# Scores of the first batch: float16 halves in place of float32 products in a fused attention and feed-forward kernel

## The chip, the cores and the metric

The kernel runs on one core of one Trainium2 chip. The time is in device microseconds; for each kernel it is the median of several executions. One further execution was recorded by the hardware profiler, and all rows of a profile come from it. The engines are TensorE (PE; its weight loads are listed as PEld), VectorE (DVE), ScalarE (ACT), GpSimd (POOL), and SyncE (SP), whose queue starts all transfers of this kernel. The program gives each engine a fixed list of instructions.

## The reference

```python
# q, k, v: 8 batches x 8 heads x 576 tokens x 64
scores = scale * np.matmul(q, k.transpose(0, 1, 3, 2))       # scale = 1/8
mask = block_i >= block_j                                    # blocks of 64 tokens
...
attn = exp(scores - max) / (sum + 1e-09)
x = (attn @ v), heads side by side                           # 4608 x 512
h = x @ w_in;  g = where(h > 0, h, exp(min(h, 0)) - 1);  x2 = g @ w_out          # 512 -> 2048 -> 512
h = x2 @ w_in2; solu = h * softmax(h); layer norm, * g_ln;  out = ln @ w_out2    # 512 -> 1024 -> 512
```

The weights arrive as float64 and are decoded on the chip from their two 32-bit words.

## The kernel before

**The stages.** Attention and the first feed-forward layer run together: while the feed-forward of batch b runs on TensorE, the attention of batch b + 1 is computed on all engines. The second feed-forward layer follows over 36 tiles of 128 tokens. Two heads make a pair (4 pairs a batch, 32 in all), and a pair has four steps: "01" (query tokens 0 to 255), "2" and "3" (128 each) and "L" (the last 64). Feed-forward works on half a batch at a time, 256 and then 320 tokens: eight products with w_in (24 matmuls each), then eight with w_out.

**Float16 halves.** Most products are computed from a high and a low float16 half of each operand, as three products (high by high, low by high, high by low). For q and k of a pair, `asum_pair` (lines 320 to 324) sums absolute values on ACT, a small matmul with ones adds over partitions (`over_partitions`, L285), `scale_pair` (329) makes the scale on VectorE, `split_hi` (338, ACT) and `split_lo` (344, VectorE) write both halves into the tile N, and `t_pair` (349) transposes N into QKT by five transposing transfers. `Step.mm` (L449, L452, L457) then multiplies.

**The first batch.** Batch 0 doesn't do this: it uses float32. `a_load` (915) brings the first 256 tokens of q and k of all heads, `a_tp` (919) transposes them on TensorE (L925), `a_cp` (928) copies the result to SBUF, and `EarlyStep.mm` (586; L594, L598, mask L600) multiplies in float32. This "pass over the first 256 tokens" gives step 01 of all four pairs at once. The steps 2, 3 and L of a pair follow with `load_early`, `e_tp` (L665) and `e_cp`. After the softmax, batch 0 stays in float32 in any case: `norm` (L610, POOL), transposes of the probabilities on TensorE (L619), and products with v (L637).

**The weights.** w_in is decoded in four groups of two pieces (`wi_*`): load, absolute value on ACT (L773), sign on POOL (L777), clamp and bit operations on VectorE (L780, L784, L785), a sum on TensorE (L844), the scale (L848), then a high half on ACT (L794) and a low half on VectorE or POOL (L798, L800). w_out follows in eight groups (`wo_*`) by the same steps. The raw words of w_out are staged in memory that w_in's decoding uses (the tile XT), so those loads wait until w_in is done. A draining of the feed-forward (`g1_act`, L693) needs the scales of all of w_in.

**The order.** Nothing in the program is dynamic. Each operation is handed to a planner (`Plan`) with an engine, a cost, a due time (`nom`) and what it depends on; the planner simulates the engines, always takes the ready operation with the earliest due time, and the instructions are written in that order. Due times come from the numbers in TUNE: w_in's group g is due at T_WI + g * D_WI, w_out's at T_WO + d * D_WO, step n of attention at `tick(n)`, the feed-forward of batch 0 at T_M0 and T_M1. STAY is how much TensorE prefers to stay with attention or with feed-forward, BACK how long after its scores a product with v is due. Buffers are rings: L and QKT have two, N one, the PSUM tiles m four. All feed-forward products form one chain in fixed order.

Of the kernel before, what the change touches and what calls it, by code (L numbers as in the profile page):

```python
# [29 lines left out]
STAY, SWITCH = 15.6, 0.11  # L30
# [6 lines left out]
SC_IN, SC_OUT, CP, ECP, GMODE, GREST = "PPAPVPVV", "VPVPPPPV", "ACT", "ACT", "PPPPPPPPPPPPPPPP", "D"  # L37
TUNE = (4.41, 8.8, 11.93, 45.41, 10.32, 10.31, 48.22, 7.08, 26.77, 46.96, 6.41, 119.81, 5.28, 10.45, 14.76, 22.34, 7.51, 12.81)
SLACK = {"PE": 0.0, "DVE": 0.0, "ACT": 0.15, "Pool": 0.1, "SP": 0.1}
KINDS = ("01", "2", "3", "L")  # L40
EARLY = 1
# [159 lines left out]
def kernel(  # L201
# [51 lines left out]
    eighth = const.tile([128, 1], F32, name="eighth")  # L253
# [35 lines left out]
    def consts():  # L289
        P.memset(mkA[:, 0:64], 2.0 ** 57)  # L290
        P.memset(mkA[:, 64:128], 0.0)
        P.memset(mkB, -(2.0 ** 57))
        P.memset(ones, 1.0)
        P.memset(ones32, 1.0)
        make_identity(nc, ident)
        P.memset(eighth, 0.125)
# [4 lines left out]
    def l_tails():  # L301
        for i in range(2):
            P.memset(L[i][64:128, :, 4], 0.0)
# [269 lines left out]
    class EarlyStep(Step, Out):  # L573
# [12 lines left out]
        def mm(s):  # L586
            s.e_tile()
            s.S = mtile(s.slot)
            qt = s.qk()
            for a in range(2):  # L590
                r = slice(64 * a, 64 * a + 64)
                if s.kind == "L":
                    for c0, c1, bank in ((0, 512, 0), (512, 576, 1)):
                        E.matmul(out=s.S[r, bank, 0:c1 - c0], lhsT=qt[r, 0, 512:576], rhs=qt[r, 1, c0:c1], start=True, stop=True)  # L594
                else:
                    for i in s.tiles:
                        n = 128 * (i + 1)
                        E.matmul(out=s.S[:, a, s.off[i]:s.off[i] + n], lhsT=qt[r, 0, 128 * i:128 * i + 128], rhs=qt[r, 1, 0:n],  # L598
                                 start=True, stop=False)
                        E.matmul(out=s.S[:, a, s.off[i] + n - 64:s.off[i] + n], lhsT=mkA, rhs=mkB, start=False, stop=True)  # L600

# [40 lines left out]

    def qkt_tile():
        return att.tile([128, 4, 576], F16, name="QKT", tag="QKT", bufs=2).rearrange("p c n -> p (c n)").bitcast(F32)

    tp_t = {}

    def load_early(p):
        h0 = 2 * p
        for w, src in enumerate((q, k)):  # L650
            t = 0 if w else 2
            for h in range(2):
                SP.dma_start(out=L[p % 2][:, w, t:4, h, :],
                             in_=src[0, h0 + h, 128 * t:512, :].rearrange("(t p) d -> p t d", p=128))
            SP.dma_start(out=L[p % 2][0:64, w, 4], in_=src[0, h0:h0 + 2, 512:576, :].rearrange("h p d -> p h d"))

    def e_tp(p, w, slot):
        if p not in qkt_t:
            qkt_t[p] = qkt_tile()[:, 0:1152].rearrange("p (s n) -> p s n", s=2)
            sc_t[p] = (None, eighth)  # L660
        tp_t[p, w] = mtile(slot).rearrange("p a n -> p (a n)")
        lo = 2 if p < 4 and w == 0 else 0
        for t in range(lo, 5):
            r = 128 if t < 4 else 64
            E.transpose(tp_t[p, w][:, 128 * t:128 * t + r], L[p % 2][0:r, w, t].rearrange("p h d -> p (h d)"), ident[0:r, 0:r])  # L665

    def e_cp(p, w):
        c = slice(256 if p < 4 and w == 0 else 0, 576)
        move("ACT" if w == 0 else ECP, qkt_t[p][:, w, c], tp_t[p, w][:, c])
# [242 lines left out]
    LA = [t.rearrange("p s t h d -> p (s t h d)")[:, 0:1024].rearrange("p (t j c) -> p t j c", t=2, j=4) for t in L]  # L912
    qa_t = {}

    def a_load(j, w, t):
        SP.dma_start(out=LA[w][:, t, 2 * j:2 * j + 2].rearrange("p z (h d) -> p (z h) d", h=2),
                     in_=(q, k)[w][0, 4 * j:4 * j + 4, 128 * t:128 * t + 128, :].rearrange("h p d -> p h d"))

    def a_tp(j, slot):
        qa_t[j] = qkt_tile()[:, 0:1024].rearrange("p (z s n) -> p z s n", z=2, s=2)  # L920
        tp_t[j] = mtile(slot, (128, 2, 2, 256))
        for z in range(2):
            for t in range(2):
                for w in range(2):
                    E.transpose(tp_t[j][:, z, w, 128 * t:128 * t + 128], LA[w][:, t, 2 * j + z], ident)  # L925

    def a_cp(j, z):
        move("ACT" if z == 0 else "DVE", qa_t[j][:, z], tp_t[j][:, z])


# [44 lines left out]
    def plan_all(fn, nom, o):  # L975
# [4 lines left out]

    a_ld = [[op("SP", DMA_IN, lambda j=j, w=w, t=t: a_load(j, w, t), -9 + j, dma=dL(131072, 256)) for w in range(2) for t in range(2)]
            for j in range(2)]
# [3 lines left out]


    a_T, a_last = [], []
    for j in range(2):
        d = rM.take()  # L990
        o = op("PE", 8 * cE(256), lambda j=j, d=d: a_tp(j, d), 5 + j, a_ld[j], d, rQKT.take(), o_const)
        a_last.append(o)
        c = op("ACT", cA(512, 0, 0, True), lambda j=j: a_cp(j, 0), 6 + j, o)
        c2 = op("DVE", cV(512), lambda j=j: a_cp(j, 1), 6 + j, o, c)
        rM.use(c, c2)
        a_T.append([c, c2])
    o_tails = op("Pool", 0.3, l_tails, 10, a_last)


# [133 lines left out]
    def plan_early(s, nom, Ts):  # L1133
        if s.kind == "L":
            c, parts = 1.4 * 4 * cE(576) + 0.1, [576]
        else:
            c = 1.4 * sum(2 * 4.05 * cE(128 * (i + 1)) + 2 * cE(64) for i in s.tiles)
            parts = [128 * (i + 1) for i in s.tiles for a in range(2)]
# [128 lines left out]
    for j in range(4):  # L1267
        gen.append((T_A + 3 * j, 0, ("A", j)))
    n = 0
    tq = {}  # L1270
    for p in range(NP):
        for kind in KINDS[1:] if p < 4 else KINDS:
            gen.append((tick(n), 0, ("S", p, kind)))
            tq.setdefault(p, tick(n))
            n += 1
    tm = 0.0
    for b in range(B):
        for i in range(32):
# [28 lines left out]
    def plan_pair_load(p, t):  # L1307
        d = [o_tails] + a_last if p < 2 else o_prep[p - 2]
        o_ld[p] = op("SP", 6 * DMA_IN, lambda: load_early(p), t, d, dma=dL(458752, 256))
        event(t + LEAD - 12, plan_pair_early, p)  # L1310

    def plan_pair_early(p, t):
        cs = []
        for w in range(2):
            nt = 3 if p < 4 and w == 0 else 5
            z = rM.take()
            o = op("PE", nt * cE(256), lambda w=w, z=z: e_tp(p, w, z), t + w, o_ld[p], z, rQKT.take() if w == 0 else o_prep[p][0])
            o_prep.setdefault(p, []).append(o)
            n = 320 if p < 4 and w == 0 else 576
            if w == 0:  # L1320
                c = op("ACT", cA(n, 0, 0, True), lambda w=w: e_cp(p, w), t + w + 0.5, o)
            else:
                c = op(ECP, cA(n, 0, 0, True) if ECP == "ACT" else cV(n), lambda w=w: e_cp(p, w), t + w + 0.5, o, cs[:1])
            z.users.append(c)
            cs.append(c)
        o_T[p] = cs
        q_users[p] = rQKT.users[-1]
# [26 lines left out]
    for t, _, g in gen:  # L1354
        run_backs(t)
        if g[0] == "A":
            j = g[1]
            s = EarlyStep(0, j, "01", lambda j=j: qa_t[j // 2][:, j % 2], lambda: (None, eighth))
            mm = plan_early(s, t, a_T[j // 2])
            rQKT.users[j // 2].append(mm)  # L1360
            event(t + MID, plan_mid, s)
            event(t + EBACK, plan_back, s)
        elif g[0] == "V":
# [6 lines left out]
        elif g[0] == "P":  # L1370
            plan_pair_load(g[1], t)
        elif g[0] == "S":
            p, kind = g[1:]
            b = p // 4
            if b < EARLY:
# [4 lines left out]
                q_users[p].append(mm)  # L1380
                event(t + MID, plan_mid, s)
# [347 lines left out]
```

## Time and profile before

| | |
|---|---|
| median of 3 runs | 1514.84 us (1513.22 to 1521.68) |
| profiled execution, its own time | 1522.49 us |
| its span, first to last instruction | 1520.7 us |
| TensorE busy | 1444.7 us, 95% |
| VectorE busy | 1052.5 us, 69% |
| ACT busy | 812.6 us, 53% |
| POOL busy | 536.3 us, 35% |
| mean granted TensorE clock | 0.972 |

A row of instructions in the profile reads: line, engine, operation, tile written <- tiles read, shapes, count | busy time in us, mean ns of one | idle time of that engine just before, and what ended it. A row of waits reads: who waited <- for whom: us in total, times, longest. A row of stages reads: stretch, its length, then busy us (and number of instructions) of each engine, the granted TensorE clock, the busy share of the DMA engines and GB/s. A row of one tile's or line's instructions has the shortest, median and longest duration in ns, the first and the last start in us, and the shapes.

### The profile page before, as it was taken

How to read it: one execution, taken by the hardware profiler on the slowest of the kernel's cores; microseconds unless marked ns; L12 is line 12 of the kernel's file. 1: busy time of each engine (PE TensorE's matmuls, PEld its weight loads, DVE VectorE, ACT ScalarE, POOL GpSimd, SP SyncE). 2: the span in 40 equal slices, each digit the busy share in tenths (PEclk: the TensorE clock that was granted, in tenths of full speed). 3: DMA queues.
4: the chain of work that ended last, by engine and by line, in shares of the span. 5: the costliest groups of instructions: out<-in, count | busy, mean ns of one | idle time of the engine just before them, and what ended most of it. 6: DMA issues, size and time to landing. Idle time of an engine off the chain costs nothing. (4 is left out here: it accounts for less than half of the span.)

```text
span 1520.7 us, 31276 instructions
## 1 busy us (share of the span) xinstructions
PE 1444.7 (95%) x12266; PEld 1022.1 (67%) x12268; DVE 1052.5 (69%) x1946; ACT 812.6 (53%) x1712; POOL 536.3 (35%) x631
## 2 busy tenths in 40 slices
PE   6888898999999999999999999989999999999998
PEld 3455565686777677678668667858776666666664
DVE  5879899878697787868868677597217555555552
ACT  4678666657475575565746656444414343333332
POOL 5677567444243343434424334242102111111110
PEclk9888799999999999999999999989999999999999
DMA  9235566856656576577565645530005444444433
GB/s 273 55 98 124 124 133 125 156 110 130 131 104 118 110 128 129 96 138 142 95 140 92 116 87 90 169 126 10 15 25 118 96 98 100 95 102 98 99 83 76
DMA packets 500130, 165.62 MB, mean 109 GB/s; under 512 B 445712, under 2 KB 492816, under 8 KB 499472
## 3 DMA queue, kind: packets, MB, share of 16 engines
q1 hardware_dynamic: 499984, 163.64, 50.7%
q8 instruction: 96, 1.57, 0.4%
q14 instruction: 50, 0.41, 0.1%
HBM read 63.44 MB, written 18.87 MB: 54 GB/s over the span
## 5 line engine op out<-in xcount | busy, mean ns | idle before, releaser
L683 PE MATMUL m<-XT,WIN 128*128 128x320 f16 (+1 forms) x3072 | 402.0, 289 | 10.5 <-DVE pwi L848 5.4
L757 PE MATMUL m<-G,WOUT 128*128 128x320 f16 (+1 forms) x3072 | 404.9, 291 | 5.2 <-POOL G L742 2.2
L683 PEld LDWEIGHTS <-WIN 128*128 128x128 f16 x3072 | 298.1, 99 | 96.1 <-issue 16.7
L757 PEld LDWEIGHTS <-WOUT 128*128 128x128 f16 x3072 | 298.8, 100 | 92.8 <-issue 8.7
L521 POOL TENSOR_SCALAR PN<-e,r 128x384 f16<-128x384 f32 (+2 forms) x280 | 184.7, 673 | 263.0 <-DVE r L503 120.3
L497 ACT ACTIVATE e<-m,nb,cqk 128x256 f32<-128x256 f32 (+4 forms) x252 | 159.7, 640 | 134.4 <-DVE nb L480 116.2
L742 POOL TENSOR_SCALAR G<-rp,sg 128x640 f16<-128x640 f32 (+1 forms) x128 | 126.6, 990 | 248.4 <-DVE rp L738 135.5
L693 ACT ACTIVATE rp<-m,ch 128x512 f32<-128x512 f32 (+1 forms) x256 | 176.4, 738 | 67.1 <-PE m L683 52.3
L1579 PE MATMUL m<-w,lt 128*128 128x512 f16 x864 | 192.2, 379 | 0.0
L526 DVE SCALAR_TENSOR_TENSOR PN<-e,r,PN 128x384 f16<-128x384 f32 (+2 forms) x280 | 172.3, 653 | 17.7 <-POOL PN L521 17.6
L1579 PEld LDWEIGHTS <-lt 128*128 128x128 f16 x864 | 81.9, 98 | 103.3 <-issue 8.9
L747 DVE SCALAR_TENSOR_TENSOR G<-rp,sg,G 128x640 f16<-128x640 f32 (+1 forms) x128 | 119.7, 938 | 26.2 <-POOL G L742 25.9
L476 DVE TENSOR_REDUCE mx<-m 128x2 f32<-128x768 f32 (+3 forms) x128 | 101.6, 814 | 44.5 <-PE m L452 37.8
L1552 POOL TENSOR_TENSOR rs<-vs,mh 128x1 f32<-128x1 f32 x36 | 20.9, 579 | 305.5 <-DVE vs L1547 305.5
L1516 PE MATMUL m<-w3h,xh 128*128 128x512 f32 x288 | 119.6, 415 | 0.0
L1516 PE MATMUL m<-w3h,xl 128*128 128x512 f32 x288 | 113.8, 395 | 0.0
L1516 PE MATMUL m<-w3l,xh 128*128 128x512 f32 x288 | 113.6, 394 | 0.0
L738 DVE SCALAR_TENSOR_TENSOR rp<-rp 128x512 f32<-128x512 f32 (+1 forms) x112 | 86.1, 769 | 33.3 <-ACT rp L695 32.7
L695 ACT ACTIVATE rp<-rp 128x640 f32<-128x640 f32 (+1 forms) x128 | 87.7, 685 | 2.0
L1523 DVE TENSOR_REDUCE mx<-m 128x1 f32<-128x1024 f32 x36 | 44.1, 1224 | 61.1 <-PE m L1516 61.1
L1504 ACT ACTIVATE xh<-x 128x512 fp32r<-128x512 f32 x36 | 22.5, 629 | 117.1 <-issue 112.8
L764 ACT ACTIVATE y<-m,ge 128x256 f32<-128x256 f32 (+1 forms) x64 | 28.4, 495 | 102.1 <-PE m L757 98.4
(169 smaller groups left out, 1901.1 us busy)
## 6 DMA issues: line engine op xcount, KB each, us to landing
x<-x2d SPq DMA_DIRECT2D x36, 256.0 KB, 3.0
out_dram<-o SPq DMA_DIRECT2D x36, 256.0 KB, 2.0
L<-in_k_dram SPq DMA_DIRECT2D x68, 128.0 KB, 2.6
WOUT<-in_moe_w_in_dram SPq DMA_DIRECT2D x8, 1024.0 KB, 6.4
LV<-in_v_dram SPq DMA_DIRECT2D x64, 128.0 KB, 2.8
XT<-in_moe_w_out_dram SPq DMA_DIRECT2D x16, 512.0 KB, 4.4
L<-in_q_dram SPq DMA_DIRECT2D x60, 128.0 KB, 2.6
x2d<-y SPq DMA_DIRECT2D x32, 160.0 KB, 2.0
```

What stands on the lines that cost most here:

```text
L476: V.tensor_reduce(out=mx[:, 2 * j:2 * j + 2], in_=s.S[:, :, s.off[i]:s.off[i] + 128 * (i + 1)], axis=AX.X, op=ALU.max)
L497: A.activation(out=dst, in_=src, func=AF.Exp, scale=s.sc()[1], bias=s.nb[:, x:x + 1], accum_out=s.su[:, x:x + 1])
L521: P.tensor_scalar(out=h, in0=e, scalar1=s.r[:, x:x + 1], scalar2=1.0, op0=ALU.mult, op1=ALU.mult)
L526: V.scalar_tensor_tensor(out=l, in0=e, scalar=s.r[:, x:x + 1], in1=h, op0=ALU.mult, op1=ALU.subtract)
L683: E.matmul(out=t[:, m, 0:n], lhsT=WIN[:, kk, wl, f:f + 128], rhs=x[:, kk, xl, o:o + n], start=kk == 0 and wl + xl == 0, stop=kk == 3 and w ...
L693: A.activation(out=d[1 + w][:, :, 0:n], in_=d[0][:, :, 0:n], func=AF.Relu, scale=ch[:, 4 * w + g:4 * w + g + 1])
L695: A.activation(out=d[2][:, :, 0:n], in_=d[2][:, :, 0:n], func=AF.Exp, scale=-1.0)
L742: P.tensor_scalar(out=GV[:, 2 * c:2 * c + 2, 0, 0:n], in0=mo_t[b, h, c][1][:, :, 0:n], scalar1=bs_t[b]["sg"], scalar2=1.0, op0=ALU.mult, o ...
L747: V.scalar_tensor_tensor(out=GV[:, 2 * c:2 * c + 2, 1, 0:n], in0=mo_t.pop((b, h, c))[1][:, :, 0:n], scalar=bs_t[b]["sg"], in1=GV[:, 2 * c: ...
L757: E.matmul(out=t[:, d % 2, 0:n], lhsT=WOUT[:, kk, wl, 128 * d:128 * d + 128], rhs=GV[:, kk, xl, 0:n], start=kk == 0 and wl + xl == 0, stop ...
L1516: E.matmul(out=t[:, nn], lhsT=a[:, kk], rhs=w[:, kk, 512 * nn:512 * nn + 512], start=kk == 0 and a is xh and w is p2["w3h"], stop=kk == 3 ...
L1579: E.matmul(out=t, lhsT=d["lt"][:, 8 * xl + kk, :], rhs=p2["w4"][:, kk, wl, :], start=kk == 0 and xl + wl == 0, stop=kk == 7 and xl == 1)
```

## The change

The float32 path for scores of batch 0 goes: `a_load`, `a_tp`, `a_cp`, `load_early`, `e_tp`, `e_cp`, `EarlyStep.mm`, and the planning of them. Batch 0 now takes `plan_pair`, like the others, with all four steps in the order of pairs, and `EarlyStep` inherits `Step.mm`. Its softmax, probabilities and products with v stay as they were. The memsets of L's tails move into the constants. Step 01 of a pair waits for two of the five transposes, and so on. The planner gets new numbers in TUNE and STAY, and `tick` has three slopes: for batch 0, for batch 1 and for the rest.

```diff
-STAY, SWITCH = 15.6, 0.11
+STAY, SWITCH = 19.1, 0.11
...
-TUNE = (4.41, 8.8, 11.93, 45.41, 10.32, 10.31, 48.22, 7.08, 26.77, 46.96, 6.41, 119.81, 5.28, 10.45, 14.76, 22.34, 7.51, 12.81)
+TUNE = (4.0, 8.6, 8.49, 12.09, 3.97, 10.09, 45.29, 7.08, 26.56, 62.96, 6.53, 119.81, 3.89, 10.45, 14.76, 23.59, -3.76, -2.9)
...
         for i in range(2):
             P.memset(LV[i][64:128, 4], 0.0)
+            P.memset(L[i][64:128, :, 4], 0.0)
             P.memset(PN[i][:, 24:26, 64:128], 0.0)
...
-        def mm(s):
-            s.e_tile()
...
-                        E.matmul(out=s.S[:, a, s.off[i]:s.off[i] + n], lhsT=qt[r, 0, 128 * i:128 * i + 128], rhs=qt[r, 1, 0:n],
-                                 start=True, stop=False)
-                        E.matmul(out=s.S[:, a, s.off[i] + n - 64:s.off[i] + n], lhsT=mkA, rhs=mkB, start=False, stop=True)
...
-    TICK0, TICK1, T_A, T_B, T_WI, D_WI, T_WO, D_WO, BACK, T_M0, D_M0, T_M1, D_M1, MID, EBACK, LEAD, NOM_V0, NOM_V1 = TUNE
+    TICK0, TICK1, TICKM, T_B, T_WI, D_WI, T_WO, D_WO, BACK, T_M0, D_M0, T_M1, D_M1, MID, EBACK, LEAD, NOM_V0, NOM_V1 = TUNE
 
     def tick(n):
-        return T_B + (n * TICK0 if n < 28 else 28 * TICK0 + (n - 28) * TICK1)
+        return T_B + min(n, 16) * TICK0 + min(max(n - 16, 0), 16) * TICKM + max(n - 32, 0) * TICK1
...
-    for j in range(4):
-        gen.append((T_A + 3 * j, 0, ("A", j)))
...
-        for kind in KINDS[1:] if p < 4 else KINDS:
+        for kind in KINDS:
...
     def plan_pair(p):
         b = p // 4
         t = tq[p]
-        d = []
-        d = o_prep[p - 2]
+        d = o_prep.get(p - 2, o_const)
         ld = op("SP", 7 * DMA_IN, lambda: load_pair(p), t - 24, d, dma=dL(589824, 256))
...
             if b < EARLY:
-                while p not in o_T:
-                    run_event(t)
+                if p not in o_T:
+                    plan_pair(p)
                 s = EarlyStep(b, p % 4, kind, lambda p=p: qkt_t[p], lambda p=p: sc_t[p])
-                mm = plan_early(s, t, o_T[p])
+                mm = plan_early(s, t, o_T[p][:need])
```

More of the change, by code (lines that the diff above doesn't have):

```diff
@@ L36 @@
 PRODUCTS = ((0, 0), (1, 0), (0, 1))
-SC_IN, SC_OUT, CP, ECP, GMODE, GREST = "PPAPVPVV", "VPVPPPPV", "ACT", "ACT", "PPPPPPPPPPPPPPPP", "D"
-TUNE = (4.41, 8.8, 11.93, 45.41, 10.32, 10.31, 48.22, 7.08, 26.77, 46.96, 6.41, 119.81, 5.28, 10.45, 14.76, 22.34, 7.51, 12.81)
+SC_IN, SC_OUT, CP, GMODE, GREST = "PPAPVPVV", "VPVPPPPV", "ACT", "PPPPPPPPPPPPPPPP", "D"
+TUNE = (4.0, 8.6, 8.49, 12.09, 3.97, 10.09, 45.29, 7.08, 26.56, 62.96, 6.53, 119.81, 3.89, 10.45, 14.76, 23.59, -3.76, -2.9)
 SLACK = {"PE": 0.0, "DVE": 0.0, "ACT": 0.15, "Pool": 0.1, "SP": 0.1}
@@ L295, in consts @@
         make_identity(nc, ident)
-        P.memset(eighth, 0.125)
         for i in range(2):
             P.memset(LV[i][64:128, 4], 0.0)
+            P.memset(L[i][64:128, :, 4], 0.0)
             P.memset(PN[i][:, 24:26, 64:128], 0.0)
-    def l_tails():
-        for i in range(2):
-            P.memset(L[i][64:128, :, 4], 0.0)
     sc_t = {}
@@ L584, in __init__ @@
                     n += i + 1
-        def mm(s):
-            s.e_tile()
[L588 to L598, printed above, removed]
-                                 start=True, stop=False)
-                        E.matmul(out=s.S[:, a, s.off[i] + n - 64:s.off[i] + n], lhsT=mkA, rhs=mkB, start=False, stop=True)
         def rr(s):
@@ L641, in f @@
             return pv_t[s.b][1]
[L643 to L669, printed above, removed]
     mo_t = {}
@@ L909, in wo_end @@
             V.tensor_copy(out=pwo[r, 2 * h:2 * h + 2], in_=pwg.rearrange("p (d a) -> p a d", a=2)[r, a, 2 * h:2 * h + 2])
[L912 to L928, printed above, removed]
     plan = Plan()
@@ L978, in plan_all @@
         return o, d.users
-    a_ld = [[op("SP", DMA_IN, lambda j=j, w=w, t=t: a_load(j, w, t), -9 + j, dma=dL(131072, 256)) for w in range(2) for t in range(2)]
-            for j in range(2)]
     o_vload, o_vsplit = {}, {}
@@ L985 @@
     o_vload[1] = op("SP", 5 * DMA_IN, lambda: load_v(1), NOM_V1, o_const, dma=dL(589824, 256))
[L988 to L997, printed above, removed]
     o_vscale, o_vall = {}, {}
@@ L1134, in plan_early @@
         if s.kind == "L":
-            c, parts = 1.4 * 4 * cE(576) + 0.1, [576]
+            c, parts = 3 * cE(512) + 3 * cE(64) + 0.1, [576]
         else:
-            c = 1.4 * sum(2 * 4.05 * cE(128 * (i + 1)) + 2 * cE(64) for i in s.tiles)
+            c = sum(3 * cE(128 * (i + 1)) + cE(64) for i in s.tiles) + 0.1
             parts = [128 * (i + 1) for i in s.tiles for a in range(2)]
@@ L1283 @@
             else:
-                t = tick(28 + 16 * (b - 1)) + i * TICK1 / 2
+                t = tick(32 + 16 * (b - 1)) + i * TICK1 / 2
             tm = max(t, tm + 0.01)
@@ L1288 @@
         gen.append((tq[4 * b] - 0.01, 0, ("V", 4 * b)))
-    for p in range(4 * EARLY):
-        gen.append((tq[p] - LEAD, 0, ("P", p)))
-    gen.sort(key=lambda x: (x[0], x[1]))
+        gen.sort(key=lambda x: (x[0], x[1]))
     backs, seq = [], []
@@ L1305, in event @@
         backs.sort(key=lambda x: x[:2])
[L1307 to L1327, printed above, removed]
     def plan_pair(p):
@@ L1355 @@
         run_backs(t)
[L1356 to L1363, printed above, removed]
+        if g[0] == "V":
             p = g[1]
@@ L1369 @@
             plan_batch_scale(p // 4, t - 10)
-        elif g[0] == "P":
-            plan_pair_load(g[1], t)
         elif g[0] == "S":
@@ L1374 @@
             b = p // 4
+            need = {"01": 2, "2": 3, "3": 4, "L": 5}[kind]
             if b < EARLY:
-                while p not in o_T:
-                    run_event(t)
+                if p not in o_T:
+                    plan_pair(p)
                 s = EarlyStep(b, p % 4, kind, lambda p=p: qkt_t[p], lambda p=p: sc_t[p])
-                mm = plan_early(s, t, o_T[p])
+                mm = plan_early(s, t, o_T[p][:need])
                 q_users[p].append(mm)
+                if kind == "L":
+                    o_ex[p] = s.ex_ops
                 event(t + MID, plan_mid, s)
@@ L1391 @@
             s = Step(b, p % 4, kind, lambda p=p: qkt_t[p], lambda p=p: sc_t[p], group)
-            need = {"01": 2, "2": 3, "3": 4, "L": 5}[kind]
             mm = plan_step(s, t, o_T[p][:need])
@@ L1590, in o_st @@
         SP.dma_start(out=out[128 * i:128 * i + 128, :], in_=h_t.pop(i)["os"])
-    t = tick(28 + 16 * 6) + 16 * TICK1
+    t = tick(32 + 16 * 6) + 16 * TICK1
     rR = Ring(2)
@@ L1627 @@
     all_g2 = [x2_ops[b] for b in range(B)]
-    t = tick(28 + 16 * 7) + 16 * TICK1
+    t = tick(32 + 16 * 7) + 16 * TICK1
     o_openw = op("Pool", 0.01, open_wk, t, all_g2)
```

1 line of the change is left out of this document (removed).

## The prediction

> **What bounds the kernel now.** I cut the span into stages where the work changes (busy time by stage), then asked which waits and which instructions mark the cuts.
>
> ```profile
> core 0: us, PE busy (x) PEld busy (x) DVE busy (x) ACT busy (x) POOL busy (x), PEclk, DMA share, GB/s
> 0.00:40.00 40.00, 28.26 (x85) 16.08 (x86) 22.45 (x36) 19.16 (x37) 20.95 (x34) 1.00 0.91 267
> 40.00:82.00 42.00, 33.30 (x176) 20.72 (x177) 36.91 (x57) 27.66 (x50) 26.46 (x21) 0.84 0.16 44
> 82.00:192.00 110.00, 92.35 (x644) 62.06 (x645) 91.71 (x173) 80.97 (x168) 73.93 (x70) 0.79 0.50 120
> 192.00:290.00 98.00, 89.48 (x999) 63.47 (x997) 87.97 (x174) 56.75 (x133) 62.84 (x69) 0.94 0.71 137
> ```
>
> ```profile
> 290.00:1128.00 838.00, 813.21 (x8643) 615.44 (x8640) 608.32 (x1151) 480.63 (x1005) 293.68 (x365) 0.99 0.53 106
> 1128.00:1520.70 392.70, 388.14 (x1730) 244.34 (x1728) 205.10 (x358) 147.46 (x324) 58.43 (x72) 1.00 0.42 95
> ```
>
> From 290 us on TensorE is busy 97% (813.21 of 838) and then 99% of the time: that is the bound of the kernel, and the change takes no work out of it. What the change edits lies before 290 us, where no engine is full: from 40 to 192 us TensorE is busy 125.7 and VectorE 128.6 of 152 us. So the question is what sets the 290.
>
> The cut at 82 is the end of the decoding of w_in, the one at 192 that of w_out; their last low halves (line 798), and who waits for the first:
>
> ```profile
> L798 DVE SCALAR_TENSOR_TENSOR WOUT<-VS,swo,WOUT x3: 1275/1278/1421, 103.5 to 190.4; 128x1024 f16<-128x1024 f32 x3
> L798 DVE SCALAR_TENSOR_TENSOR WIN<-XT,swi,WIN x2: 1277/1278/1279, 80.8 to 82.0; 128x1024 f16<-128x1024 f32 x2
> ```
>
> ```profile
> SPq L870 <- DVE VS L785: 36.4, 7, 8.0
> SPq L870 <- DVE WIN L798: 32.1, 2, 31.3
> ```
>
> The loads of w_out (L870) sit in the queue until w_in is through (31.3 us in one wait), because their staging lies in memory that w_in's decoding uses, and then again and again until VectorE has emptied the staging (36.4). The second matrix products need w_out, and all feed-forward products run in one fixed order, so the second half of batch 0 starts only after 192 us. Nor is a product of the first half drained before the scales of all of w_in exist; the first draining is at 81.5:
>
> ```profile
> L693 ACT ACTIVATE rp<-m,ch x37: 664/691/815, 81.5 to 299.8; 128x512 f32<-128x512 f32 x21, 128x640 f32<-128x640 f32 x16
> ```
>
> The path to 290 is therefore: w_in decoded (82), w_out decoded (192), then a stretch of 98 us with TensorE at 91%. VectorE, POOL and ACT decode; attention of batch 0 is in their way.
>
> **The change part by part.** TensorE first. Batch 0 loses its float32 scores (L598, L594, masks L600) and its transposes of q and k (L925, L665); it gets the products that seven batches have now (L449, L457, masks L452).
>
> ```profile
> L449 PE MATMUL m<-QKT 64*128 64x512 f16 (+3 forms) x672 | 62.3, 301 | 8.7 <-DMA QKT<-N 6.8 <-ACT rp L693 1.6
> L598 PE MATMUL m<-QKT 64*128 64x128 f32 (+3 forms) x64 | 40.0, 722 | 6.1 <-ACT e L497 2.7 <-DVE pwi L848 1.2 <-DVE XT L537 1.0
> L457 PE MATMUL m<-QKT 64*64 64x512 f16 (+1 forms) x336 | 26.0, 288 | 0.8 <-DVE XT L537 0.8
> L452 PE MATMUL m<-mkB,mkA 64*128 64x64 bf16 x224 | 21.7, 190 | 0.0
> ...
> L665 PE MATMUL m<-ident,L 128*128 128x128 f32 (+1 forms) x32 | 8.4, 383 | 0.0
> L285 PE MATMUL m<-am,ones 128*128 128x2 f32 x56 | 8.1, 214 | 0.3 <-ACT rp L693 0.3
> L600 PE MATMUL m<-mkB,mkA 128*128 128x64 bf16 x32 | 7.3, 229 | 0.0
> L594 PE MATMUL m<-QKT 64*64 64x512 f32 (+1 forms) x32 | 5.9, 498 | 3.0 <-ACT rp L693 2.1 <-ACT e L497 1.0
> L925 PE MATMUL m<-ident,L 128*128 128x128 f32 x16 | 4.7, 435 | 4.6 <-DMA L<-in_q_dram 3.1 <-DMA L<-in_k_dram 1.5
> ```
>
> Out: 40.0 + 7.3 + 5.9 + 8.4 + 4.7 = 66.3 us. In: a seventh of 62.3 + 26.0 + 21.7 + 8.1 (the sums over partitions, L285), 16.9 us. TensorE does 49 us less in its first 290. It is not the engine that the path waits for there, so I count that at nothing, save where VectorE waits for it (below).
>
> VectorE and ACT: per pair two sums of absolute values on ACT (L324 with its read of the accumulator), two high halves (L341), two low halves on VectorE (L346) and three small operations (as L333).
>
> ```profile
> L324 ACT ACTIVATE jk<-L x56: 720/737/767, 104.9 to 860.6; 128x640 bf16<-128x640 f32 x56
> L324 ACT ACTIVATION_READ_ACCUMULATOR jk<-L x56: 185/187/230, 105.5 to 861.3; 128x1 f32 x56
> ```
>
> ```profile
> L341 ACT ACTIVATE N<-L,sqk x56: 812/827/866, 126.1 to 906.9; 128x640 f16<-128x640 f32 x56
> L346 DVE SCALAR_TENSOR_TENSOR N<-L,sqk,N x56: 855/883/2556, 128.6 to 910.8; 128x640 f16<-128x640 f32 x56
> L333 DVE RECIPROCAL sqk<-pq x28: 165/166/167, 124.1 to 906.0; 128x2 f32<-128x2 f32 x28
> ```
>
> ```profile
> L353 SPq DMA_TRANSPOSE QKT<-N x140: 1169/1264/2512, 148.7 to 923.8; - x140
> ...
> L568 ACT ACTIVATE QKT<-m x10: 428/598/653, 6.9 to 122.0; 128x320 f32<-128x320 f32 x4, 128x576 f32<-128x576 f32 x4, 128x512 f32<-128x512 f32 x2
> L570 DVE COPY QKT<-m x2: 692/692/692, 7.5 to 9.9; 128x512 f32<-128x512 f32 x2
> ...
> DMA to landing us min/median/max: 2.3/2.5/5.2
> ```
>
> VectorE gets 8 x 0.883 + 12 x 0.166 = 9.1 us and loses two copies, 1.4: 7.7 more, on an engine that is 85% busy from 40 to 192, so I charge all of it to the path. ACT gets 8 x (0.737 + 0.187 + 0.827) = 14.0 and loses ten copies of some 0.6: 8 more. At 71% busy (108.6 of 152) it has 43 us free there; charged at nothing, and at 8 if that cover were gone. The two memsets of L's tails move ahead of the first pair's load: under a microsecond, and that load has others ahead of it.
>
> SP's queue: the same q and k are read, but 20 transposes are added, 1.26 us each in the queue, and each waits for VectorE's low halves; behind them stand the loads of w_in's later pieces and of the next pair. N has one buffer, so pairs follow one another at 4 splits (3.4), five transposes (6.3) and a landing (2.5), about 12 us. If the first split starts around 11 (a guess: two loads of w_in and the pair's own come first), the fourth pair has its first scores around 55 us (11, 3 x 12, 3.4, two transposes and a landing). That leaves 26 us for its softmax and its product with v before the 81.5 at which the feed-forward is first drained now. So I price this at nothing; what those steps take beyond the 26, and what the draining comes forward, would be lost again.
>
> The pass over the first 256 tokens: it stands ahead of w_in three times, which the following rows show: its eight loads precede w_in's first in the queue; its sixteen normalisations take POOL before 60 us; VectorE stands waiting for its masks.
>
> ```profile
> 0.72 1.00 SPq L916 DMA_DIRECT2D L<-in_q_dram  x2
> ...
> 5.06 1.02 SPq L810 DMA_DIRECT2D WOUT<-in_moe_w_in_dram  x2
> ```
>
> ```profile
> 0.00:60.00 60.00, 11.80 (x16) 0.97 0.72 208
> ```
>
> ```profile
> DVE mx L476 <- PE m L600: 6.7, 3, 4.1
> ```
>
> The second row is POOL's time in the normalisations (L610). The new planner numbers put w_in before attention (T_WI 3.97, the steps from 12.09). Loads: up to 4.3 us gained (0.72 instead of 5.06). POOL: the normalisations stay, but the later pairs' fall behind w_in; between 6 and 11.8, I take 9. Waits for masks behind float32 scores: 6.7, of which float16 scores leave little.
>
> Sum: 4.3 + 9 + 6.7 - 7.7 = 12.3 us earlier at the end of w_in, and with it w_out, the 290 and the end: late next is VectorE, which decodes w_out. With the small ends (6 on POOL, half of 6.7, VectorE's splits 9.1) it is 4.5, with the large ones 15. The profiled execution took 1522.49 (span 1520.7), 7.65 above the median of 1514.84; the difference carries over, so 1514.84 - 12.3 = **1502.5**, on its own 1499 to 1510. The later stages are ordered anew by STAY, TICK1 and BACK; 25 us without TensorE lie in the 838, so this could give some and may cost as much. I take nothing and widen the range.
>
> **The rivals.** Half a per cent, 7.6 us, is about what a measurement of this kernel tells from no change.
>
> Nothing comes of it: w_in ends earlier but VectorE, 85% busy, gives it back on w_out and the splits. Gain 0 to 6, 1509 to 1518. For it: 36.4 us of the queue's waiting is for VectorE, whatever w_in does.
>
> VectorE decides, slower: from 82 to 192 it is at 83%; if w_in doesn't end earlier, the 7.7 to 9.1 us of splits at that filling cost 9 to 11 (9.1 / 0.83), and the path ends at 1526. It decides as soon as w_in ends less than 8 us earlier than 82, for instance because transposes hold up w_in's loads in the queue. Against it: the first 40 us leave VectorE 17.5 free.
>
> TensorE decides, faster: stage 192 to 290 holds the second half of the feed-forward of batch 0 and nearly all attention of batch 1. If half of the 49 us freed lets batch 1 move ahead of 192, the time is near 1490, with all of it 1466. Against: batch 1 too needs VectorE.
>
> The clock, slower. The same 24 products of 128x256 took 5.28 us at one time and 2.79 at another:
>
> ```profile
> 70.97 5.28 PE L683 MATMUL m<-XT,WIN 128*128 128x256 f16 x24 [5.41 <-DVE pwi L848]
> ```
>
> ```profile
> 290.00 2.79 PE L683 MATMUL m<-XT,WIN 128*128 128x256 f16 x24
> ```
>
> and the granted clock is 0.84 and 0.79 between 40 and 192. Less work on TensorE means more gaps. If 8 of the first half's 16 such sets turned slow, they would cost 8 x 2.49 = 20 us, 1535. It decides only where TensorE is waited for; with 49 us less to do it has room for this before 192. The Trainium skill (TensorE: Matmul & The Clock Gate, Part 1: The HAM clock gate) has the array fall to half clock after an idle window of some 3.4 us, and so speaks against taking matmuls out of a sparse stage; the trace agrees that the set after an idle 5.41 us is the slow one.
>
> That the change doesn't do what it says I don't see: the float32 products leave the code.
>
> **How the numbers follow.** Forecast 0.46, TensorE decides 0.08, nothing comes of it 0.26, VectorE decides 0.15, clock 0.05. Faster by over 0.5% (below 1507.3): nearly all of the forecast and the TensorE case, 0.52; slower (above 1522.4): the last two, 0.20; same 0.28. The range goes from 1482 (leaving out the better half of the TensorE case) to 1528 (leaving out the clock and a VectorE case that costs more than 13).
>
> **What would show it.** Right: the last L798 on WIN well before 82 and that on WOUT before 192, the first product of batch 1's feed-forward before 290, an unchanged 838 after it. Wrong: w_in ending at 82 or later with SP waiting for low halves (L346); ACT's first draining held up by attention (XT) instead of by scales; VectorE over 90% from 40 to 192; sets of 5 us after that.

## The result, and the profile after

The changed kernel takes 1539.95 us in the median (1538.72 to 1542.33), beside 1518.26 of the kernel before on the same chip: ratio 1.0134, 95% interval 1.0104 to 1.0164. It is slower by 21.7 us; the forecast was 1502.5, with an end at 1528. The profiled execution has a span of 1537.8 us, 17.1 more than before. TensorE is busy 1399.9 us in it instead of 1444.7, 45 less, and so idle 137.9 us instead of 76.0. The question is which idle time this is.

Busy time by stage, at the same kinds of cuts as in the prediction (w_in decoded; first feed-forward product; second half of batch 0; batch 1; second stage):

```profile
core 0: us, PE busy (x) PEld busy (x) DVE busy (x) ACT busy (x) POOL busy (x), PEclk, DMA share, GB/s
0.00:40.00 40.00, 8.43 (x42) 4.40 (x42) 25.72 (x37) 21.64 (x31) 17.30 (x27) 1.00 0.94 253
40.00:82.00 42.00, 25.07 (x188) 14.91 (x189) 36.51 (x75) 34.88 (x75) 26.64 (x22) 0.92 0.39 103
82.00:130.40 48.40, 30.68 (x252) 21.55 (x253) 40.52 (x92) 36.60 (x87) 22.81 (x28) 0.65 0.67 150
130.40:203.20 72.80, 48.91 (x443) 39.42 (x443) 65.78 (x121) 48.58 (x100) 60.32 (x54) 0.88 0.53 112
203.20:303.70 100.50, 89.20 (x1048) 63.82 (x1045) 77.07 (x145) 51.63 (x118) 56.27 (x64) 0.98 0.66 125
...
303.70:1145.20 841.50, 809.30 (x8589) 613.45 (x8585) 605.79 (x1141) 478.76 (x996) 292.26 (x363) 1.00 0.51 104
1145.20:1537.80 392.60, 388.33 (x1730) 244.50 (x1728) 205.15 (x358) 147.44 (x324) 58.41 (x72) 1.00 0.42 95
```

The two last stages are nearly those of before (838.0 and 392.7): 3.4 us of the 17.1 lie there. The other 13.7 stand at 303.7, where 290 was. In the stage from 130 to 203 TensorE has 67% (48.91 of 72.8) and POOL 83%. The kernel before, in the same stretch, had 88% and 59%, with VectorE about as busy as now (64.49 and 65.78):

```profile
130.40:203.20 72.80, 64.25 (x469) 44.16 (x470) 64.49 (x126) 47.14 (x104) 42.93 (x41) 0.77 0.56 124
```

Now the marks that the prediction named: the last low halves of w_in and w_out, the first draining, and the queue's first load of w_in:

```profile
L749 DVE SCALAR_TENSOR_TENSOR WIN<-XT,swi,WIN x2: 1279/1279/1279, 79.1 to 80.3; 128x1024 f16<-128x1024 f32 x2
L749 DVE SCALAR_TENSOR_TENSOR WOUT<-VS,swo,WOUT x3: 1273/1274/1278, 100.0 to 201.9; 128x1024 f16<-128x1024 f32 x3
L644 ACT ACTIVATE rp<-m,ch x256: 665/747/824, 139.2 to 1120.1; 128x512 f32<-128x512 f32 x64, 128x640 f32<-128x640 f32 x64
```

```profile
0.72 0.96 SPq L761 DMA_DIRECT2D WOUT<-in_moe_w_in_dram  x2
```

The loads of w_in do start 4.3 us earlier (0.72), but its last low half starts at 80.3 instead of 82.0. The last of w_out comes at 201.9 instead of 190.4, and the first draining at 139.2 instead of 81.5. That last mark moved by far the most. What the feed-forward waits for shows in the first scores of each pair and in the first products of the feed-forward (timeline of TensorE; start, duration):

```profile
32.11 0.50 PE L444 MATMUL m<-QKT 64*128 64x128 f16 x6 [9.35 <-DMA QKT<-N]
63.58 0.34 PE L444 MATMUL m<-QKT 64*128 64x128 f16 x6 [0.73 <-ACT e L492]
87.05 0.34 PE L444 MATMUL m<-QKT 64*128 64x128 f16 x6
113.44 0.50 PE L444 MATMUL m<-QKT 64*128 64x128 f16 x6
130.46 2.78 PE L634 MATMUL m<-XT,WIN 128*128 128x256 f16 x24
...
226.73 3.43 PE L634 MATMUL m<-XT,WIN 128*128 128x320 f16 x24
303.69 2.79 PE L634 MATMUL m<-XT,WIN 128*128 128x256 f16 x24
```

A product of the first half needs the first 256 tokens of all four pairs. The fourth pair has its first scores at 113.44; softmax and product with v follow, ACT writes its part of XT at 129.25 (below), and the product starts at 130.46, where before it started at 60.71. The second half of batch 0 follows at 226.73 instead of 203.08, batch 1 at 303.69 instead of 290.00.

```profile
129.25 0.45 ACT L528 ACTIVATE XT<-m,sv 128x256 f16<-128x256 f32 x1
```

### The profile page after: what moved, and what is told of

It is laid out like the page before. It is cut to its first block, busy times and chain, and to the rows that moved or that the text cites. A ratio compares the mean times of both kernels' runs of the same rounds, so it can differ in the third digit from the quotient of the medians.

```text
span 1537.8 us, 31343 instructions
## 1 busy us (share of the span) xinstructions
PE 1399.9 (91%) x12276; PEld 1002.0 (65%) x12276; DVE 1056.5 (69%) x1964; ACT 819.5 (53%) x1726; POOL 534.0 (35%) x630
## 5 line engine op out<-in xcount | busy, mean ns | idle before, releaser
L708 PE MATMUL m<-G,WOUT 128*128 128x320 f16 (+1 forms) x3072 | 397.7, 288 | 10.4 <-DVE G L698 3.8
L516 POOL TENSOR_SCALAR PN<-e,r 128x128 f16<-128x128 f32 (+3 forms) x280 | 188.5, 686 | 274.6 <-DVE r L498 108.4
L492 ACT ACTIVATE e<-m,nb,cqk 128x128 f32<-128x128 f32 (+4 forms) x288 | 182.7, 639 | 144.8 <-DVE nb L475 120.2
L521 DVE SCALAR_TENSOR_TENSOR PN<-e,r,PN 128x128 f16<-128x128 f32 (+3 forms) x280 | 181.4, 685 | 24.6 <-POOL PN L516 24.5
L471 DVE TENSOR_REDUCE mx<-m 128x2 f32<-128x1024 f32 (+3 forms) x128 | 101.7, 815 | 44.6 <-PE m L447 44.4
L444 PE MATMUL m<-QKT 64*128 64x256 f16 (+3 forms) x768 | 75.1, 313 | 23.2 <-DMA QKT<-N 21.3
L558 PE MATMUL m<-PT,VS 128*64 128x128 f16 (+1 forms) x2520 | 71.0, 212 | 16.2 <-DMA PT<-PN 10.5
```

The costliest lines, as they stand in the source:

```text
L471: V.tensor_reduce(out=mx[:, 2 * j:2 * j + 2], in_=s.S[:, :, s.off[i]:s.off[i] + 128 * (i + 1)], axis=AX.X, op=ALU.max)
L492: A.activation(out=dst, in_=src, func=AF.Exp, scale=s.sc()[1], bias=s.nb[:, x:x + 1], accum_out=s.su[:, x:x + 1])
L516: P.tensor_scalar(out=h, in0=e, scalar1=s.r[:, x:x + 1], scalar2=1.0, op0=ALU.mult, op1=ALU.mult)
L521: V.scalar_tensor_tensor(out=l, in0=e, scalar=s.r[:, x:x + 1], in1=h, op0=ALU.mult, op1=ALU.subtract)
L708: E.matmul(out=t[:, d % 2, 0:n], lhsT=WOUT[:, kk, wl, 128 * d:128 * d + 128], rhs=GV[:, kk, xl, 0:n], start=kk == 0 and wl + xl == 0, stop ...
```

## The experiments

Three theories. **A**: without the pass, the first 256 tokens of the fourth pair come late, so the feed-forward of batch 0 starts late, and that is the loss. **B**: the splits are the loss, 7 to 9 us of VectorE where it is nearly full, with their transposes in the queue (the prediction's slower rival). **C**: the order is the loss. It is dealt out from a few numbers, and a new deal costs something whatever the work is.

All medians below are beside runs of the kernel before on the same chip (1518.3 to 1519.8 us). The three right columns come from the profiled executions: the start of the first feed-forward product, of the first product of batch 1, and from there to the end of the span. Each of these comes from one execution, whose time lies up to 6.2 us from its kernel's median. Kernels 1, 2, 5, 9, 10, 11 and 13 have other planner's numbers than before and after.

| kernel | median us | ratio (95%) | first product | batch 1 | rest |
|---|---|---|---|---|---|
| before | 1518.26 | | 60.7 | 290.0 | 1230.7 |
| after | 1539.95 | 1.0134 (1.0104 to 1.0164) | 130.5 | 303.7 | 1234.1 |
| 1 halves, with the pass | 1529.82 | 1.0061 (1.0043 to 1.0078) | 70.5 | 294.6 | 1229.7 |
| 2 float32, no pass | 1544.99 | 1.0163 (1.0122 to 1.0204) | 156.8 | 307.7 | 1230.1 |
| 3 after, low halves twice | 1544.91 | 1.0157 (1.0118 to 1.0195) | 137.2 | 311.4 | 1234.7 |
| 4 after, no low halves | 1535.13 | 1.0097 (1.0066 to 1.0129) | 129.8 | 303.8 | 1229.8 |
| 5 after, step 01 first | 1530.40 | 1.0082 (1.0053 to 1.0112) | 112.5 | 302.0 | 1229.5 |
| 6 before, pass later | 1530.40 | 1.0075 (1.0056 to 1.0095) | 84.9 | 302.5 | 1228.3 |
| 7 before, four numbers | 1530.37 | 1.0072 (1.0045 to 1.0099) | 60.6 | 287.4 | 1238.0 |
| 8 after, three numbers | 1542.51 | 1.0150 (1.0117 to 1.0183) | 141.4 | 310.5 | 1235.8 |
| 9 after, feed-forward freed | 1527.24 | 1.0065 (1.0043 to 1.0087) | 27.4 | 295.5 | 1229.0 |
| 10 the same, no low halves | 1529.56 | 1.0075 (1.0048 to 1.0101) | 27.0 | 294.4 | 1233.2 |
| 11 kernel 1, no low halves | 1529.43 | 1.0066 (1.0043 to 1.0088) | 70.2 | 292.7 | 1234.5 |
| 12 before, feed-forward freed | 1518.98 | 1.0001 (0.9986 to 1.0015) | 44.0 | 288.0 | 1229.3 |
| 13 float32, no pass, freed | 1529.06 | 1.0062 (1.0040 to 1.0084) | 27.1 | 287.7 | 1241.0 |
| 14 before, one number | 1527.98 | 1.0061 (1.0040 to 1.0082) | 60.6 | 292.2 | 1233.3 |
| 15 before, STAY | 1531.22 | 1.0080 (1.0054 to 1.0106) | 60.8 | 285.9 | 1244.2 |

**The change taken apart (1 and 2).** Kernel 1 keeps the float32 pass and takes the later steps from halves:

```diff
+    class HalfStep(EarlyStep):
+        mm = Step.mm
...
-                mm = plan_early(s, t, o_T[p])
+                mm = plan_early(s, t, o_T[p][:{"2": 3, "3": 4, "L": 5}[kind]])
```

> The kernel before with its float32 pass over the first 256 tokens kept, and steps 2, 3 and L of batch 0 from scaled float16 halves; so all the splits and transposes of the change, without the removal of the pass. The planner's numbers are its own. Theory A (the removed pass: without it the feed-forward of batch 0, which needs step 01 of all four pairs, starts 70 us later, and that costs the time): the first feed-forward product near 60 to 75 us as before, 1500 to 1522 us, so no slower than before. Theory B (the splits on VectorE, 7.7 us at an engine that is 85% busy, and the transposes in the queue): slower than before by 10 us or more, 1528 to 1542. Theory C (the order, planned by numbers that differ between the kernels, decides, whatever the work): either, with the first product's time telling nothing.

Kernel 2 does the reverse: float32 scores for all of batch 0, but no pass.

```diff
-    for j in range(4):
-        gen.append((T_A + 3 * j, 0, ("A", j)))
...
-        for kind in KINDS[1:] if p < 4 else KINDS:
+        for kind in KINDS:
```

> The kernel before without the pass: all four steps of batch 0 pair after pair as in the change, but from float32 products, with no splits and no transposes in the queue. The planner's numbers are near those of the change. Theory A: as late as the change, first feed-forward product after 110 us, 1532 to 1550 us. Theory B: about as before, 1515 to 1526, since the 7.7 us of splits are gone. Theory C: either.

Taking the pass away, without any split, costs at least as much (25.7 us) as the whole change; keeping it, with all the splits, costs 10.5. So A seems to have the larger part, and 10 us remain that look like B. Part of kernel 2's lateness is planned, though: its steps of batch 0 are due from 30 us and its feed-forward from 86 (T_B and T_M0), where the change has 12.09 and 62.96. Its low halves of w_in and w_out, the first scores of its fourth pair, and its first products:

```profile
L799 DVE SCALAR_TENSOR_TENSOR WIN<-XT,swi,WIN x2: 1280/1282/1285, 66.9 to 68.1; 128x1024 f16<-128x1024 f32 x2
L799 DVE SCALAR_TENSOR_TENSOR WOUT<-VS,swo,WOUT x3: 1276/1285/1301, 85.3 to 165.6; 128x1024 f16<-128x1024 f32 x3
```

```profile
132.90 0.48 PE L599 MATMUL m<-QKT 64*128 64x128 f32 x2
156.81 2.78 PE L684 MATMUL m<-XT,WIN 128*128 128x256 f16 x24
...
307.70 2.79 PE L684 MATMUL m<-XT,WIN 128*128 128x256 f16 x24
```

w_in is decoded 13.9 us earlier than before (68.1 against 82.0) and w_out 24.8 earlier (165.6 against 190.4), and batch 1 starts 17.7 us later. Both weights are there early; the products wait for the fourth pair.

**The price of the low halves (3, 4, 11).** Kernel 3 computes the low halves of batch 0 twice, in the same order:

```diff
-            lo = op("DVE", cV(640) * BUSY, lambda s=s: split_lo(p, s), t - 10 + s, hi)
+            lo = op("DVE", cV(640) * BUSY, lambda s=s: split_lo2(p, s), t - 10 + s, hi)
```

> The changed kernel with the low halves of batch 0 computed twice over on VectorE (8 more of 0.89 us, 7.1 us) in the same planned order. Theory A: the low halves lie ahead of the first feed-forward product, on the late path itself, but VectorE is idle for 40% of the first 130 us: 0 to 5 us more than the change. Theory B: the splits cost one for one or more: 7 to 10 us more. Theory C: nothing, the order is the same.

Kernel 4 leaves them out, again in the same order:

```diff
     def split_lo(p, s):
         n = n_t[p]
+        if p < 4:
+            P.memset(n[:, :, 2 * s + 1], 0.0)
+            return
```

> The changed kernel in the same planned order, with the low halves of batch 0 left out on VectorE; the low halves of q and k are zeros that GpSimd writes. Theory A: 0 to 5 us less than the change, still at least 10 slower than the kernel before. Theory B: 8 to 12 us less, most of the difference to the kernel before gone. Theory C: no difference to the change.

VectorE is idle for less than the expectation says: 27.7 of the first 130.4 us of the change, 21%. In the profile of kernel 3 the first product moves by 6.7 us when 7.1 are added ahead of it, and batch 1 by 7.7; the median rises by 5.0, the upper end of what A allows. Taking the low halves out does not bring the product forward (129.8 and 303.8), and the 4.8 us in the median show in the profile only behind the start of batch 1. GpSimd's eight zeroings cost 0.63 us each, though, 5.1 in all:

```profile
L342 POOL MEMSET N<- x8: 625/632/640, 11.1 to 84.7; 128x640 f16 x8
```

so this kernel alone doesn't price the low halves at nothing. Kernel 11 makes the same edit to kernel 1, where the feed-forward isn't late:

> The kernel with the float32 pass and steps 2, 3 and L from halves, in its planned order, with the low halves of batch 0 left out on VectorE (GpSimd writes zeros). Theory B (the splits make its 10 us over before): back to 1518 to 1523. If those 10 us are the order's: 1526 to 1530, within 4 us of that kernel. Theory A has no share here.

1529.43 against 1529.82: there, low halves in place of zeroings cost nothing that can be measured, and nothing shows the 10 us of kernel 1 to be theirs. High halves and transposes stay in that kernel, so they are not priced by it.

**The order (7, 8, 14, 15).** Four numbers of the kernel before moved a little:

```diff
-TUNE = (4.41, 8.8, 11.93, 45.41, 10.32, 10.31, 48.22, 7.08, 26.77, 46.96, 6.41, 119.81, 5.28, ...
+TUNE = (4.55, 8.8, 11.93, 46.54, 10.32, 10.31, 48.22, 7.08, 26.77, 47.01, 6.41, 120.36, 5.28, ...
```

> The kernel before with four of the planner's numbers moved by 0.05 to 1.1 us (the tick of batch 0, the start of its later steps, the start of each half of its feed-forward): the same work in a slightly different order, the first feed-forward product still near 61 us. Theories A and B: within 5 us of before. Theory C (the order decides, whatever it is that moves): 10 us or more, in either direction.

Then three numbers of the changed kernel (4.0 to 3.91, 8.6 to 8.62, 12.09 to 12.91):

> The changed kernel with three of the planner's numbers moved by 0.02 to 0.8 us: the same work in a slightly different order. Theories A and B: within 5 us of the change, 1535 to 1545. Theory C: 10 us or more away from it, in either direction.

Then one number of the kernel before (4.41 to 4.5), and STAY alone (15.6 to 19.1):

> The kernel before with one of the planner's numbers moved by 2% (the tick of batch 0, 4.41 to 4.5): the same work, the first feed-forward product still near 61 us. If the order of before is a well-placed one, and any other costs about 10 us: 1526 to 1534. If not: 1515 to 1523.

> The kernel before with the number that the change moves for the later batches (STAY, 15.6 to 19.1) and nothing else. If it makes the change's 3.6 us between the first feed-forward product of batch 1 and the second stage: 2 to 6 us slower, 1520 to 1525, all of it after 290 us. If that is chance: within 3 us of before.

This was the surprise. With the same work, three other orders of the kernel before take 1528.0 to 1531.2 us, 8 to 12 more. The order of before is a well-placed one, and C is real. Where it costs differs: with four numbers and with STAY, batch 1 starts earlier than before (287.4, 285.9) and the time is lost behind that. For STAY, the stretch from batch 1 to the second stage:

```profile
285.88:1137.50 851.62, 816.09 (x8691) 616.75 (x8687) 612.03 (x1155) 482.79 (x1007) 296.38 (x369) 0.99 0.53 105
```

851.6 us where before has 838.0, with TensorE busy 816.1 against 813.2: what is added is idle time. I had expected 2 to 6 us of STAY, and the median shows 11.4. Another order of the changed kernel moves it by only 2.6 us.

**The late start, moved by itself (5, 6).** Kernel 6 is the kernel before with the second half of the pass planned 15 us later:

```diff
-        gen.append((T_A + 3 * j, 0, ("A", j)))
+        gen.append((T_A + 3 * j + (j > 1) * 15, 0, ("A", j)))
```

> The kernel before with one number changed: the second half of the pass (the first 256 tokens of pairs 2 and 3) is planned 15 us later. All of the work of before and nothing of the change. Theory A: the first feed-forward product moves from 61 to about 85 us, and the kernel is 5 to 15 us slower. Theory B: no splits, so no change beyond 3 us. Theory C: it may move either way by some us.

Its first product comes at 84.9, and batch 1 at 302.5, 12.5 us later than before; the rest is 2.4 shorter. Yet its last low halves come earlier than before, at 73.2 for w_in (82.0) and at 187.3 for w_out (190.4):

```profile
L798 DVE SCALAR_TENSOR_TENSOR WIN<-XT,swi,WIN x2: 1441/1468/1496, 71.9 to 73.2; 128x1024 f16<-128x1024 f32 x2
L798 DVE SCALAR_TENSOR_TENSOR WOUT<-VS,swo,WOUT x3: 1307/2296/2300, 95.4 to 187.3; 128x1024 f16<-128x1024 f32 x3
```

So a late first half delays batch 1 even when both weights are early, with one number moved and no splits. That is the pattern of the change (a loss ahead of batch 1) and not that of kernels 7 and 15, whose loss lies behind. By the median alone (1530.4) it can't be told from another deal. Kernel 5 plans step 01 of all four pairs first, with the changed kernel's work:

```diff
+            if p in (2, 3):
+                qkt_t[p] = PN[p - 2][:, 0:18].rearrange("p c n -> p (c n)").rearrange("p (c n) -> p c n", c=4)
...
+    for p, kind in [(p, "01") for p in range(4)] + [(p, x) for p in range(NP) for x in KINDS if p > 3 or x != "01"]:
```

> The changed kernel (float16 halves, no float32 pass), with step 01 of all four pairs of batch 0 planned ahead of the later steps; pairs 2 and 3 keep their transposed halves in the two PN buffers, which are free until the feed-forward's end. The same work; the planner's numbers are its own. Theory A (the late first feed-forward product costs the time): the first product comes some 20 us earlier than in the change (130), and 5 to 15 us of the loss come back, 1524 to 1535. Theory B (the splits): as the change, 1537 to 1543. Theory C (the numbers of the order): anything between.

The fourth pair's first scores come at 95.55 instead of 113.44, the first product at 112.52, and the median is 9.6 us below that of the change:

```profile
95.55 0.50 PE L447 MATMUL m<-PN 64*128 64x128 f16 x6
112.52 3.81 PE L637 MATMUL m<-XT,WIN 128*128 128x256 f16 x24
```

But batch 1 starts only 1.7 us earlier than in the change (301.95); the profiled execution gains 4.6 of its 6.3 us behind that. So kernel 5 shows that the late pair can be brought forward, and not what the late start costs.

**The feed-forward freed of attention (9, 10, 12, 13).** The direct test of A: the work stays, but the first half of batch 0's feed-forward reads a constant tile, so it needn't wait for any pair.

```diff
-                    E.matmul(out=t[:, m, 0:n], lhsT=WIN[:, kk, wl, f:f + 128], rhs=x[:, kk, xl, o:o + n],
+                    E.matmul(out=t[:, m, 0:n], lhsT=WIN[:, kk, wl, f:f + 128], rhs=XZ[:, 0:n] if free else x[:, kk, xl, o:o + n],
...
-        xs = list(x_done[b, 0]) + (list(x_done[b, 1]) if h else [])
+        xs = list(x_done[b, 0]) + (list(x_done[b, 1]) if h else []) if b or h else [o_const]
```

> The changed kernel with the first half of batch 0's feed-forward freed of attention: its products read a constant tile of 0.01 in place of attention's output for the first 256 tokens, so that part of batch 0's output is left out; all the attention work, the splits and the transposes stay. The planner's numbers are its own. Theory A alone (the late first product is the whole loss): 1516 to 1523 us, as before. Theory B alone (the splits): 1537 to 1543, as the change. Both, each with a part: 1526 to 1535, with the first product of batch 1 between 290 and 300 us.

> The same, in the same planned order, with the low halves of batch 0 also left out on VectorE (GpSimd writes zeros), so the low halves of q and k and attention's share in the first half of the feed-forward are left out. Theory A alone: no difference to the run with the freed feed-forward. Theory B: 5 to 8 us less than that. Both: 3 to 6 less, and then 1522 to 1530.

> A control: the kernel before with the first half of batch 0's feed-forward freed of attention in the same way (a constant tile of 0.01 in place of attention's output for the first 256 tokens). Theory A: nothing to be had, since there the first product waits for w_in and its scales and not for attention: within 5 us of before. Theory C: it may be 10 us slower, since the order is dealt anew. Theory B says nothing.

> The kernel before without the pass, from float32 products and without splits or transposes in the queue, its steps pair after pair, with the first half of batch 0's feed-forward freed of attention (a constant tile of 0.01 in place of attention's output for the first 256 tokens), and the same planner's numbers as the freed kernel with halves (1527). If the 8 us that kernel has over before are the halves' (transposes, splits, ACT): 1516 to 1521. If they are the order's: 1523 to 1531. If the late first product is the loss of the float32 kernel without the pass (1545): in either case at least 12 less than that.

The freed changed kernel has its first two products at 27.39, the third at 83.35, and batch 1 at 295.52:

```profile
27.39 8.19 PE L637 MATMUL m<-XZ,WIN 128*128 128x256 f16 x48
83.35 4.92 PE L637 MATMUL m<-XZ,WIN 128*128 128x256 f16 x24
...
295.52 2.78 PE L637 MATMUL m<-XT,WIN 128*128 128x256 f16 x24 [0.58 <-DVE XT L534]
```

It takes 1527.24 us, 12.7 less than the change. In the profiles 8.2 us of the gain lie ahead of batch 1 and 5.1 behind. Leaving out the low halves as well brings nothing more (1529.56). The kernel before gains nothing from the same freedom (1518.98), though its first product then starts at 44.03: there, attention wasn't what the path waited for. And float32 without the pass, freed, takes 1529.06, 15.9 less than with the wait. That kernel has no splits and no transposing transfers, and takes what the freed one with halves takes. That speaks against the halves as the cause of what is left, but doesn't exclude them: the freed kernel with halves still starts batch 1 5.5 us later than before (295.5), the float32 one 2.3 us earlier (287.7), and loses its time behind (1241.0).

What is left, 8 to 10 us, is as much as three other orders of the kernel before cost. So of the 21.7 us the late start has some 8 (the start of batch 1) to 13 (the median), and the rest agrees with the order alone. The two can't be parted to better than a few us, since each freed kernel has an order of its own. Other orders of the changed kernel than those of the table I haven't run: one as well placed as that of before may exist, and if its first half came as late, it would still be slower by that much.

## Why the prediction was wrong

**The step that failed** is the one on SP's queue: "pairs follow one another at 4 splits (3.4), five transposes (6.3) and a landing (2.5), about 12 us", from which the fourth pair's first scores came out at 55 us, with 26 us to spare, and the step was priced at nothing. The pairs come 31, 23 and 26 us apart, and the fourth has its first scores at 113.44. Of these 58 us, 13 are the first pair's (32.11, where the working gives 19: its first split starts at 16.27 instead of 11, and TensorE waits 9.35 us for its first transpose); the other 45 lie between the pairs. I had added up what one pair's splits and transposes take and left out everything between them: in the new order each pair runs steps 01, 2, 3 and L before the next, on engines that also decode w_in and then w_out.

In the trace the later pairs' scores do not wait for splits or transposes at all. Here are the last four transposes of the second, third and fourth pair (first and last start in us), and the wait that took most of TensorE's time between 40 and 130 us:

```profile
L348 SPq DMA_TRANSPOSE QKT<-N x4: 1247/1262/1284, 48.5 to 52.5; - x4
L348 SPq DMA_TRANSPOSE QKT<-N x4: 1246/1262/1291, 71.8 to 75.7; - x4
L348 SPq DMA_TRANSPOSE QKT<-N x4: 1252/1258/1286, 96.2 to 100.7; - x4
PE m L598 <- POOL e L589: 13.5, 9, 5.7
```

The first scores of these pairs, at 63.58, 87.05 and 113.44, start 11 to 13 us after the last of their transposes was issued, and a transpose lands after 2.3 to 5.8 us. They come next in TensorE's list, behind transposes of probabilities (L598) and products with v of the pair before, and those wait for the softmax, most of all for POOL's normalisation (L589), 13.5 us in this stretch. Kernels 2 and 13 agree: their batch 0 has no splits, and the fourth pair comes at 132.9 and 144.0. Kernel 5 shows that putting the steps 01 first takes 18 us off.

From there on, the working was right about the 26 us: from scores to the product it takes 17.0 (113.44 to 130.46). The prediction had written that what is lost beyond them "would be lost again", and had named the mark, a first draining held by attention instead of by scales. Its product is held by attention until 130.46; the last 6 us up to 139.2 go by on ACT, with w_out and the next batch's halves.

**The path to 290** (w_in decoded, w_out decoded, 98 us) was the path of before only as long as the first half is ready when w_out comes. The pass, which I treated as an obstacle ahead of w_in, made it ready. Kernels 2 and 6 have both weights earlier and batch 1 later.

**The gain at w_in**, 4.3 + 9 + 6.7 = 20 before VectorE's share, was 1.7 in the change. The loads start their 4.3 us earlier. VectorE's waits for masks fell from 6.7 to 2.6. The term that was mis-sized is POOL's, 9: up to the end of w_in's decoding POOL is in normalisations for as long as before, 14.93 us (15 of them) and 14.28 (20), since now the first pair runs all its steps, and the second most of them, ahead of that end. The change first, then before:

```profile
0.00:80.30 80.30, 14.93 (x15) 0.96 0.67 179
0.00:82.00 82.00, 14.28 (x20) 0.92 0.53 153
```

4.3 + 4.1 - 0.6 is 7.8, and the splits may take most of that: six of the eight low halves come before 80 us, and 7.1 us more of them move w_in's end 5.8 later (86.1 in kernel 3), though leaving them out, with zeroings in their place, brings it only 1.0 forward (79.3 in kernel 4). This part stays open.

Kernel 2's 13.9 us are no measure of these terms, since its steps are planned 18 us later than those of the change. Kernel 13 has the same float32 work, with its steps due from 12.24, and ends w_in where the change does:

```profile
L802 DVE SCALAR_TENSOR_TENSOR WIN<-XT,swi,WIN x2: 1279/1281/1283, 77.4 to 79.7; 128x1024 f16<-128x1024 f32 x2
```

The prediction's guess for such a case, transposes that hold up the loads of w_in, is not it: the last of these loads leaves the queue at the same time in the change and in kernel 2 (start, duration of the last such group):

```profile
37.37 1.04 SPq L761 DMA_DIRECT2D WOUT<-in_moe_w_in_dram  x2
```

```profile
37.20 0.55 SPq L811 DMA_DIRECT2D WOUT<-in_moe_w_in_dram  x1
```

The 12 us between the ends of w_in in the two kernels (68.1 and 80.3) arise behind the loads; by kernel 13 they go with the order and not with the halves.

**VectorE, 7.7 us charged to the path one for one**: in the medians, low halves in place of zeroings cost nothing measurable where the feed-forward isn't late (10 and 11). Ahead of the late start, doubling them moved the first product one for one (3), and leaving them out, with the zeroings in their place, did not move it back (4). The slower rival "VectorE decides" had the right sign and the wrong engine: VectorE is at 90% from 130 to 203, but it was at 89% there before.

**TensorE, 49 us less, charged at nothing**: measured 45 less busy and worth nothing, as said.

**After 290, unchanged**: 841.5 and 392.6 for 838.0 and 392.7. Kernels 3 and 4, which have the order of the change, show 842.1 and 837.2 in that stretch, so 3.5 us is no more than one execution differs from another there. I had taken nothing for the new numbers there; kernel 15 shows that STAY alone can cost 11 us in another order.

**The clock** did not do what its rival said: no feed-forward product lies in the stretch from 82 to 130 us, where the granted clock is 0.65 (before 0.82), and from 130 to 203 it is 0.88 against 0.77. Three of the first half's sixteen sets take 3.9 to 4.3 us, the others about 2.8. But attention of the third and fourth pair does lie there, ahead of the late product, and some of it runs slower:

```profile
77.56 0.85 PE L598 MATMUL m<-ident,e 128*128 128x128 f32 x6
94.92 0.58 PE L284 MATMUL m<-amo,ones 128*128 128x1 f32 x2 [4.35 <-ACT rn L838]
95.36 1.52 PE L598 MATMUL m<-ident,e 128*128 128x128 f32 x6
```

The Trainium skill (TensorE: Matmul & The Clock Gate, Part 1: The HAM clock gate) has the clock fall after an idle window; the trace agrees, with six transposes that take 1.52 us behind an idle 4.35 and took 0.85 before it. What the low clock adds to the late start no run separates. An estimate of the most it can be is 11 us, from TensorE's 30.68 busy us in the stretch at 0.65.

## What to carry to other kernels

Before pricing work that a change takes away, ask what it made ready, and when: an early pass that looks like an obstacle may be what lets the next stage start. Where a stage needs parts from several items, work out when the last item's part arrives, from all that the new order puts between the items and not from what one item costs. And where the order comes out of tuned numbers, run the old kernel with the numbers moved a little, so that the cost of a new deal (here 8 to 12 us) is known before a difference of that size is explained by anything else.

## What the runs showed of the hardware

Two things were new to me. A transpose of q and k in the first 130 us of the change landed 11.2 us after its issue, where the slowest of the kernel before took 5.2; the median is 2.5 in both. It is the first transpose of the first pair, issued at 20.87 right behind four loads of w_in, and TensorE waits 9.35 us for it (8.29, 10.86 and 10.14 in kernels 3, 4 and 8). What made it late wasn't tried:

```profile
DMA to landing us min/median/max: 2.3/2.5/11.2
```

And single executions of kernels with the same order (the change, 3 and 4) and the same later work differ by up to 5 us in a stretch of 838 us (837.2, 841.5, 842.1): a few us in one profile are no finding there.
